# Linear attention and a SiLU feed-forward in one kernel: how the last 64 rows of each weight are loaded, and where four mask operations stand

## The chip, the cores and the metric

One core of a Trainium2 chip runs the whole program. The metric is the device time of one execution in microseconds. Engines are named as in the profile: PE (TensorE, matmuls and weight loads), DVE (VectorE), ACT (ScalarE), POOL (GpSimd), SP (SyncE, which here only issues transfers). Transfers are issued from two queues, SP's and ACT's, and run on 16 DMA engines.

## What is computed

```python
def _A_ref(x, wqkv, w_phi, wo):              # B=1, S=2048, D=448, H=16, Dh=28
    qkv = (x @ wqkv).reshape(B, S, 3, H, Dh).transpose(2, 0, 3, 1, 4)
    q, k, v = qkv[0], qkv[1], qkv[2]
    pq = einsum("bhsd,hdf->bhsf", q, w_phi)
    pk = einsum("bhsd,hdf->bhsf", k, w_phi)
    phi_q = concatenate([softmax(pq), softmax(-pq)], axis=-1)
    phi_k = concatenate([softmax(pk), softmax(-pk)], axis=-1)
    kv = einsum("bhsf,bhsd->bhfd", phi_k, v)
    z = einsum("bhsf->bhf", phi_k)
    num = einsum("bhqf,bhfd->bhqd", phi_q, kv)
    den = einsum("bhqf,bhf->bhq", phi_q, z)[..., None] + 1e-6
    o = num / den
    return o.transpose(0, 2, 1, 3).reshape(B, S, D) @ wo

def _B_ref(x, w1, w2):                       # w1 448 x 1792, w2 1792 x 448
    return silu(x @ w1) @ w2

xn = layernorm(x)
out = x + _A_ref(xn, wqkv, w_phi, wo) + _B_ref(xn, w1, w2)
```

All tensors are bfloat16.

## The kernel before

The 2048 tokens are worked on in eight pairs of 128-token tiles (`p` from 0 to 7). The depth of 448 is kept as seven blocks of 64 rows, and matmuls run as two half-array matmuls of 64 rows each, one on partitions 0 to 63 and one on 64 to 127 (`mm_448`, line 497). For that every weight stands in SBUF twice. The first 384 rows come in one load of 128 partitions times three blocks (`load_main`, line 566), and a copy of each half is written to the other half by DVE or ACT (`swap`, line 575; tile `w_sb` of the profile for w1). The last 64 rows, the tail, are loaded by `load_tail` (line 569) twice, once to partitions 0 to 63 and once to 64 to 127; no swap touches them.

The stages, in order: layer norm of a pair (`ln_pair`, line 672: statistics on DVE at line 621, the reciprocal root on POOL at 637, the normalised tile `xn_sb` at 650, a transpose on PE for pairs 0 to 3 at 508 and on the DMA for later ones); the first feed-forward product of pairs 0 to 3 (`ffn1_chunk`, 14 f-tiles of 128 columns, silu on ACT); the product of `w_phi` into wq and wk (`fold`); for each pair keys, values, their exponentials, sums and normalised features (`k_macro`, line 791), then one group of queries; every second pair the products of key features and values (`k_acc`, line 812); then the attention output, the second feed-forward product and wo. While PE has nothing to do at the start it multiplies zeros (`warm`, tile `zz`).

In `k_macro` the value copy out of PSUM is line 800 (DVE), the sums of the exponentials line 805 (DVE), their reciprocal 807 (DVE) and the product of features and reciprocal 808 (POOL). `k_acc` of pairs p-2 and p-1 stands behind the query group of pair p, for p of 2, 4 and 6, and reads the results of line 808.

The mask constants: POOL makes `maskh` (lines 524 and 527), DVE copies two columns of it to both halves of `mask2` (line 532, twice) and from there to the last column of `KVZ` (line 537, twice). They are read for the first time at line 862, when the key-value sums are done.

The order of work on each engine is not written out: each operation is recorded with its reads, writes, an assumed duration and a priority (`cur_prio`, 0 first), and `schedule` (line 218) plays the program through and picks operations by when they could start, by priority and by order of recording. For loads it reckons landing times ahead (`plan`, lines 247 to 272) from bytes and assumed rates, and adds 1700 ns to each. The order that comes out is fixed in the program; each engine then waits on semaphores. The loads of one queue are issued in the order of recording (lines 583 to 607): on SP x0, w1_0 (columns 0 to 255), x1, w1_0b (256 to 511), w1_1 (512 to 1023), the tail of columns 512 to 1791 as two loads, w1_2a (1024 to 1407), w1_2b (1408 to 1791), x2, x3, w_phi, then the transposed loads of wq and wk, x4 to x7, wv and its tail (`wvt`), wo's tail (`wot`); on ACT the two loads of the tail of columns 0 to 511. x0 is pair 0, x1 pair 1, and so on.

Of the kernel before, what the change touches and what calls it, by code (L numbers as in the profile page):

```python
# [144 lines left out]
class _Prog:  # L145
# [72 lines left out]
    def schedule(self):  # L218
        ops = self.ops
# [27 lines left out]
        plan = {}  # L247
# [5 lines left out]
        now, stalled = 0.0, False  # L253
        while loads["sp"] or loads["act"]:
            live = [e for e in ("sp", "act") if loads[e] and loads[e][0][2] <= now]
            nxt = [loads[e][0][2] for e in ("sp", "act") if loads[e] and loads[e][0][2] > now]
            if not live:
                now = min(nxt)
                continue
            cap = [190.0 if ops[loads[e][0][0]].half or ops[loads[e][0][0]].name == "wT_dt" else 310.0 for e in live]  # L260
            rates = [min(c, 310.0 * c / sum(cap)) for c in cap]
            step = min(min(loads[e][0][1] / r for e, r in zip(live, rates)), min(nxt) - now if nxt else 1e18)
            now += step
            if now > 2350.0 and not stalled:
                stalled = True
                now += 900.0
            for e, r in zip(live, rates):
                q = loads[e][0]
                q[1] -= step * r
                if q[1] <= 1.0:  # L270
                    plan[q[0]] = now + 1700.0
                    loads[e].pop(0)

        ndeps = [len(o.deps) + len(o.odeps) for o in ops]
# [25 lines left out]
        while done < n:  # L300
            cands = []
            tmin = None
            for e in ENGINES:
                for oid in ready[e]:
                    o = ops[oid]
# [11 lines left out]
            _, t, o = best  # L317
# [6 lines left out]
            if fill is not None:  # L324
                _, t, o = fill
# [39 lines left out]
def bass_parallel_sum__linear_kernel_hedgehog__dense_activation_silu__prompt_kernel(  # L365
# [10 lines left out]
    S, D, H, DH, FF = 2048, 448, 16, 28, 1792  # L376
# [9 lines left out]
    with es:  # L386
        def sb(name, shape, dt):
            return es.enter_context(nc.sbuf_tensor(name, shape, dt))
# [8 lines left out]
        w1_sb = sb("w1_sb", [128, KB, FF], BF16)  # L397
# [27 lines left out]
        KVZ = sb("KVZ", [128, 2, G, 2, DH + 2], BF16)  # L425
        kvs = sb("kvs", [128, 8 * 2 * (DH + 1)], F32)
        mask2 = sb("mask2", [128, 2], F32)
# [5 lines left out]
        maskh = sb("maskh", [KP, 4], F32)  # L433
# [30 lines left out]
        P = _Prog()  # L464
# [7 lines left out]
        def d_dve(n, mode=1):  # L472
            return n * 1.042 / mode + 150.0

        def d_rec(n):
            return n * 6.25 + 150.0

        def d_pool(n, per=1.0):
            return n * per + 120.0
# [34 lines left out]
        def act(dst, src, func, name, table=None, scale=1.0):  # L514
            return P.op("act", d_act(_cols(src)), lambda e: e.activation(dst, src, func, scale=scale),  # L515
                        reads=[src], writes=[dst], table=table, name=name)
# [4 lines left out]
             reads=[ones_bf[:]], writes=[ident[:]], name="ident")  # L521
# [4 lines left out]
             reads=[ones4[:]], writes=[mtmp[:]], name="mask1")  # L526
        P.op("pool", d_pool(4), lambda e: e.affine_select(maskh[:], mtmp[:], [[DH, 4]], ALU.is_ge, 0.0,
                                                           base=DH - 1, channel_multiplier=-1),
             reads=[mtmp[:]], writes=[maskh[:]], name="mask2")
        P.cur_prio = 2  # L530
        for r in range(2):
            P.op("dve", 150, lambda e, r=r: e.tensor_copy(mask2[64 * r:64 * r + 56, :], maskh[0:56, 0:2]),  # L532
                 reads=[maskh[0:56, 0:2]], writes=[mask2[64 * r:64 * r + 56, :]], name="mask3")
        for r in range(2):
            kvz_ones = KVZ[64 * r:64 * r + 56].rearrange("p s g h c -> p (s g) h c")[:, :, :, DH + 1]
            m2 = mask2[64 * r:64 * r + 56]
            P.op("dve", 150, lambda e, k=kvz_ones, m2=m2: e.tensor_copy(k, m2[:, None, :].broadcast_to([56, 8, 2])),  # L537
                 reads=[m2], writes=[kvz_ones], name="kvz1")
        wpad = W_sb[:, :, 0:QW].rearrange("p k (j f) -> p k j f", f=64)[:, :, :, 56:64]
        P.op("pool", d_pool(KB * 64), lambda e: e.memset(wpad, 0.0), writes=[wpad], name="wpad")  # L540

# [1 line left out]
        table_op = act(mtmp[:, 0:1], ones4[:, 0:1], ACTF.Silu, "table", table="silu")  # L543
# [10 lines left out]
        def load(dst, src, nbytes, name, eng="sp", keys_r=(), half=False):  # L554
            return P.dma(lambda e: e.dma_start(out=dst, in_=src), nbytes, writes=[dst], name=name, eng=eng, keys_r=keys_r, half=half, dur=580.0)
# [7 lines left out]
        def load_x(p0, p1, eng="sp"):  # L563
            load(x_sb[:, 2 * p0:2 * p1, :].rearrange("p (q t) d -> p q t d", t=2), xt[:, p0:p1], (p1 - p0) * 256 * D * 2, f"x{p0}", eng)

        def load_main(dst, src, c0, c1, d0, name):
            load(dst[:, 0:3, d0:d0 + c1 - c0], src[0:384, c0:c1].rearrange("(k p) f -> p k f", p=128), 384 * (c1 - c0) * 2, name)

        def load_tail(dst, src, c0, c1, d0, name, eng="sp"):
            for h in range(2):  # L570
                o = load(dst[64 * h:64 * h + 64, d0:d0 + c1 - c0], src[384:448, c0:c1], 64 * (c1 - c0) * 2, name, eng, half=True)
                if eng == "act":
                    o.odeps.add(table_op.id)

        def swap(dst, c0, c1, engs):
            for h in range(2):
# [6 lines left out]
        load_x(0, 1)  # L583
        load_main(w1_sb, B_w1, 0, 256, 0, "w1_0")
        load_tail(w1_sb[:, 6], B_w1, 0, 512, 0, "w1_0t", "act")
        load_x(1, 2)
        load_main(w1_sb, B_w1, 256, 512, 256, "w1_0b")
        load_main(w1_sb, B_w1, 512, 1024, 512, "w1_1")
        load_tail(w1_sb[:, 6], B_w1, 512, FF, 512, "w1_1t")
        load_main(w1_sb, B_w1, 1024, 1408, 1024, "w1_2a")  # L590
        load_main(w1_sb, B_w1, 1408, FF, 1408, "w1_2b")
        load_x(2, 3)
        load_x(3, 4)
# [126 lines left out]
        def exp_act(dst, src, scale, name):  # L720
            o = act(dst, src, ACTF.Exp, name, table="exp", scale=scale)
            for s in silus:
                if s.id not in o.deps:
                    o.odeps.add(s.id)
            exps.append(o)
# [61 lines left out]
        def k_unit(p, j, b0, name):  # L787
            mm_448([banks[b0 + t][:, 0:D] for t in range(2)], lambda h, k: xnT[:, k, p, :],
                   lambda h, k: W_sb[:, k, KO + (j - 1) * D:KO + j * D], True, True, name + "_mm", okeys_w=("late",) if p == NPAIR - 1 and j == 2 else ())

        def k_macro(p):
            sl = p % NEK
            k_unit(p, 1, 0, "pk")
            kb = psum[:, 0:1024].rearrange("p (t c) -> p t c", t=2)[:, :, 0:D]
            for s in range(2):
                exp_act(Ek[:, sl, :, s, :], kb, 1.0 if s == 0 else -1.0, "exp_k")
            k_unit(p, 2, 2, "v")
            vb = psum[:, 1024:2048].rearrange("p (t c) -> p t c", t=2)[:, :, 0:D].rearrange("p t (h d) -> p t h d", h=H)
            dstv = vaug[:, sl, :, :, 0:DH]
            P.op("dve", d_dve(896), lambda e: e.tensor_copy(dstv, vb), reads=[vb], writes=[dstv], name="v_ev")  # L800
            for ts in ((0, 2),) if p < NPAIR - 1 else ((0, 1), (1, 2)):
                n = ts[1] - ts[0]
                E3 = Ek[:, sl, ts[0]:ts[1], :, :].rearrange("p t s (h f) -> p (t s h) f", f=DH)
                S3, R3 = Sk[:, sl, 32 * ts[0]:32 * ts[1]], Rk[:, sl, 32 * ts[0]:32 * ts[1]]
                P.op("dve", d_dve(896 * n), lambda e, S3=S3, E3=E3: e.tensor_reduce(S3, E3, AXL.X, ALU.add),  # L805
                     reads=[E3], writes=[S3], name="Sk")
                P.op("dve", d_rec(32 * n), lambda e, S3=S3, R3=R3: e.reciprocal(R3, S3), reads=[S3], writes=[R3], name="Rk")  # L807
                P.op("pool", d_pool(896 * n, 1.77), lambda e, E3=E3, R3=R3, n=n: e.tensor_tensor(  # L808
                    E3, E3, R3[:, :, None].broadcast_to([128, 32 * n, DH]), ALU.mult),
                    reads=[E3, R3], writes=[E3], name="phik")  # L810
# [25 lines left out]
        for sl in range(NEK):  # L836
            P.op("pool", d_pool(32), lambda e, sl=sl: e.memset(vaug[:, sl, :, :, DH], 1.0),
                 writes=[vaug[:, sl, :, :, DH]], name="vaug1")
        for p in range(NPAIR):
            k_macro(p)  # L840
            if 1 <= p <= 5:
                P.keyw["early"] = exps[-1].id
                late_loads(p - 1)
            q_group(p // 4, p % 4)
            if p in (2, 4, 6):
                k_acc(p - 2, p)
# [3 lines left out]
        for r in range(2):  # L850
            lo, hi = 64 * r, 64 * r + 56
            src = [banks[4 + h][lo:hi, 0:464] for h in range(2)]
            dst = kvs[lo:hi, :]
            P.op("dve", d_dve(464), lambda e, src=src, dst=dst: e.tensor_copy(dst, src[0]), reads=[src[0]], writes=[dst], name="kvs")  # L854
            P.op("dve", d_dve(464), lambda e, src=src, dst=dst: e.tensor_tensor(dst, src[1], dst, ALU.add),  # L855
                 reads=[src[1], dst], writes=[dst], name="kvs2")
        for r in range(2):
            lo, hi = 64 * r, 64 * r + 56
            dst = KVZ[lo:hi, :, :, :, 0:DH + 1].rearrange("p s g h c -> p (s g) h c")
            src = kvs[lo:hi, :].rearrange("p (q h c) -> p q h c", q=8, h=2)  # L860
            m2 = mask2[lo:hi]
            P.op("dve", d_dve(464), lambda e, src=src, dst=dst, m2=m2: e.tensor_tensor(  # L862
                dst, src, m2[:, None, :, None].broadcast_to([56, 8, 2, DH + 1]), ALU.mult),
                reads=[src, m2], writes=[dst], name="kvz")
# [137 lines left out]
        p = NPAIR - 2  # L1002
# [7 lines left out]
        ops = P.ops  # L1010
# [12 lines left out]
        for e in ("pe", "act", "dve", "pool"):  # L1023
            cnt = 0
            for oid in order[e]:
                o = ops[oid]
# [4 lines left out]
        for e in ENGINES:  # L1031
            for oid in order[e]:
                o = ops[oid]
# [88 lines left out]
```

## Time and profile before

| | us |
|---|---|
| median of 3 runs | 158.16 |
| the runs | 158.72, 158.16, 157.37 |
| the profiled execution | 157.24 |
| its span in the profile | 155.5 |

| engine | busy us | share of the span |
|---|---|---|
| PE | 150.7 | 97% |
| PE weight loads | 98.3 | 63% |
| DVE | 102.6 | 66% |
| ACT | 74.2 | 48% |
| POOL | 63.7 | 41% |

The busy shares over 40 slices of 3.9 us each, with the DMA engines' (a digit is tenths, 9 is 90% or more):

```profile
PE   6889999999999999999999999999999999999994
DVE  5897977995978875889098769667985930022042
POOL 5320306379388775479601453366146060000000
PEclk9999999999999999999999999999999999999999
DMA  5999678303724223300000083300840143041011
```

Read these as averages over stages with different limits: PE is full from the third slice on, and the DMA engines are full in the first three slices. Two idle times are named in the view of waits: POOL waits 18.1 us in six pieces for DVE's line 635 in the first 30 us, and DVE waits 0.4 us for x to land.

### The profile page before, as it was taken

The page shows a single profiled execution, that of the slowest core. Times are in us where ns is not written, and L with a number is a line of the kernel's source. Part 1 is how long each engine was busy: PE and PEld are TensorE (multiplying, and loading weights), DVE is VectorE, ACT ScalarE, POOL GpSimd, SP SyncE. Part 2 cuts the span into 40 slices and gives each one's busy share as a digit, 9 for nine tenths or more (in the row PEclk, how much of TensorE's full clock was granted, in tenths as well). Part 3 has the DMA queues.
Part 4 walks back from the last instruction along what each step waited for, and adds up shares of the span by engine and source line. Part 5 has one row for each costly group of instructions (what it writes and reads, how often), then busy time and mean ns, then how long its engine had stood idle before and what let it go on. Part 6 is the DMA issues. An engine that isn't in the chain of part 4 may idle for free.

```text
span 155.5 us, 6049 instructions
## 1 busy us (share of the span) xinstructions
PE 150.7 (97%) x2751; PEld 98.3 (63%) x2751; DVE 102.6 (66%) x198; ACT 74.2 (48%) x82; POOL 63.7 (41%) x73
## 2 busy tenths in 40 slices
PE   6889999999999999999999999999999999999994
PEld 2378899795444546446878898655555555556553
DVE  5897977995978875889098769667985930022042
ACT  3778757878789688785955566800000000000000
POOL 5320306379388775479601453366146060000000
PEclk9999999999999999999999999999999999999999
DMA  5999678303724223300000083300840143041011
GB/s 152 268 277 115 110 180 249 62 17 69 99 53 139 49 93 95 93 0 6 4 4 4 0 63 63 59 4 0 124 118 4 28 115 98 0 118 63 0 59 59
DMA packets 23353, 12.11 MB, mean 78 GB/s; under 512 B 16160, under 2 KB 23200, under 8 KB 23328
## 3 DMA queue, kind: packets, MB, share of 16 engines
q1 hardware_dynamic: 23168, 11.60, 34.9%
q8 instruction: 21, 0.34, 0.9%
q10 hardware_dynamic: 160, 0.13, 0.3%
q14 instruction: 4, 0.03, 0.1%
HBM read 6.22 MB, written 1.84 MB: 52 GB/s over the span
## 4 chain that ended last, share of the span: by engine, by line
PE 89%; DVE 7%; POOL 2%; issue 1%; POOLq 0%
PE psum L490 84%; PE psum L483 4%; PE psum L508 1%; DVE st L621 1%; POOL rstd L637 1%; DVE KVZ L862 1%; DVE kvs L854 1%; DVE kvs L855 1%; DVE mask L532 1%; DVE xn_sb L650 1%; DVE mv L629 0%; DVE xnT L668 0%; DVE ve L635 0%; DVE KVZ L537 0%; POOL ident L519 0%
## 5 line engine op out<-in xcount | busy, mean ns | idle before, releaser
L490 PE MATMUL psum<-xnT,w_sb 64*128 64x256 bf16 (+1 forms) x1008 | 45.6, 246 | 0.5 <-DVE xn_sb L650 0.5
L490 PEld LDWEIGHTS psum<-xnT,w_sb 64*128 64x128 bf16 x1008 | 39.2, 94 | 5.0 <-ACT w_sb L515 0.6
L515 ACT ACTIVATE ar<-psum 128x896 bf16<-128x896 f32 (+2 forms) x38 | 32.0, 880 | 10.9 <-PE psum L490 10.8
L916 POOL TENSOR_TENSOR scr<-scr 128x384 bf16<-128x384 f32 (+3 forms) x32 | 20.1, 660 | 31.8 <-DVE scr L911 26.0
L808 POOL TENSOR_TENSOR ar<-ar,Rk 128x1792 bf16<-128x1792 bf16 (+1 forms) x9 | 25.8, 2877 | 10.1 <-DVE Rk L807 9.1
L960 DVE TENSOR_TENSOR out_sb<-psum,x_sb 128x448 bf16<-128x448 f32 (+2 forms) x17 | 9.5, 593 | 23.6 <-PE psum L490 20.5
L490 PE MATMUL psum<-ar,xnT 64*128 64x448 bf16 x224 | 22.7, 349 | 0.0
L490 PE MATMUL psum<-w_sb,hT_lo 64*128 64x448 bf16 x224 | 22.3, 349 | 0.0
L515 ACT ACTIVATE eq<-psum 128x1024 bf16<-128x1024 f32 x16 | 15.5, 1025 | 6.1 <-PE psum L490 6.0
L805 DVE TENSOR_REDUCE Sk<-ar 128x64 f32<-128x1792 bf16 (+1 forms) x9 | 16.2, 1804 | 2.5 <-ACT ar L515 2.5
L490 PEld LDWEIGHTS psum<-ar,xnT 64*128 64x128 bf16 x224 | 10.7, 94 | 10.4 <-DVE ar L800 0.4
L911 DVE TENSOR_TENSOR scr<-psum,Gq 128x896 f32<-128x896 f32 x16 | 16.9, 1087 | 0.4
L515 ACT ACTIVATE hT_lo<-psum 128x1024 bf16<-128x1024 f32 x14 | 14.3, 1022 | 5.9 <-PE psum L490 5.9
L490 PE MATMUL psum<-w_sb,ar 64*128 64x448 bf16 x168 | 16.6, 349 | 0.0
L490 PEld LDWEIGHTS psum<-w_sb,hT_lo 64*128 64x128 bf16 x224 | 10.5, 94 | 9.4
L637 POOL TENSOR_TENSOR rstd<-ve,neghalf 128x2 f32<-128x2 f32 (+1 forms) x9 | 6.2, 690 | 21.3 <-DVE ve L635 18.9
L490 PE MATMUL psum<-xnT,ar 64*128 64x512 bf16 x112 | 13.4, 376 | 0.0
L490 PEld LDWEIGHTS psum<-w_sb,ar 64*128 64x128 bf16 x168 | 8.4, 94 | 7.4
L490 PE MATMUL psum<-wo_sb,scr 64*128 64x448 bf16 (+2 forms) x119 | 11.9, 338 | 0.0
L800 DVE CAST ar<-psum 128x896 bf16<-128x896 f32 x8 | 8.6, 1069 | 4.0 <-PE psum L490 4.0
L621 DVE BATCH_NORM_STATS2 st<-x_sb 128x6 f32<-128x448 bf16 x16 | 9.7, 613 | 0.5 <-DMA x_sb<-in_A_x_dram 0.4
L650 POOL TENSOR_SCALAR xn_sb<-x_sb,mv,rstd 128x192 bf16<-128x192 bf16 (+1 forms) x8 | 9.5, 1190 | 0.4
(50 smaller groups left out, 119.4 us busy)
## 6 DMA issues: line engine op xcount, KB each, us to landing
out_dram<-out_sb SPq DMA_DIRECT2D x7, 224.0 KB, 2.2
x_sb<-in_A_x_dram SPq DMA_DIRECT2D x4, 224.0 KB, 5.4
x_sb<-in_A_x_dram SPq DMA_DIRECT2D x2, 448.0 KB, 4.8
w_sb<-in_B_w_dram SPq DMA_DIRECT2D x2, 448.0 KB, 3.6
w_sb<-in_B_w_dram SPq DMA_DIRECT2D x2, 336.0 KB, 3.4
w_sb<-in_B_w_dram SPq DMA_DIRECT2D x2, 288.0 KB, 6.6
w_sb<-in_B_w_dram SPq DMA_DIRECT2D x2, 192.0 KB, 3.4
w_sb<-in_B_w_dram SPq DMA_DIRECT2D x1, 384.0 KB, 6.5
```

Of the source, the lines that this page charges most:

```text
L483: lambda e: e.matmul(dst, lhsT, rhs, start=start, stop=stop, skip_group_check=True),
L490: r = e.matmul(dst, lhsT, rhs, start=start, stop=stop, skip_group_check=True)
L515: return P.op("act", d_act(_cols(src)), lambda e: e.activation(dst, src, func, scale=scale), reads=[src], writes=[dst], table=table, name= ...
L621: o = P.op("dve", 630, lambda e: e.bn_stats(st6[:, t, :], x_sb[:, t, :]), reads=[x_sb[:, t, :]], writes=[st6[:, t, :]], name="bnst")
L637: P.op("pool", 580, lambda e: e.tensor_tensor(r2, v2, nh, ALU.pow), reads=[v2, nh], writes=[r2], name="rstd")
L650: o = P.op("pool" if pool else "dve", 150 + _cols(xs) * 1.6 if pool else 120 + _cols(xs) * 0.6, lambda e, xn=xn, xs=xs: e.tensor_scalar(xn ...
L800: P.op("dve", d_dve(896), lambda e: e.tensor_copy(dstv, vb), reads=[vb], writes=[dstv], name="v_ev")
L805: P.op("dve", d_dve(896 * n), lambda e, S3=S3, E3=E3: e.tensor_reduce(S3, E3, AXL.X, ALU.add), reads=[E3], writes=[S3], name="Sk")
L808: P.op("pool", d_pool(896 * n, 1.77), lambda e, E3=E3, R3=R3, n=n: e.tensor_tensor(E3, E3, R3[:, :, None].broadcast_to([128, 32 * n, DH]), ...
L911: P.op("dve", d_dve(896), lambda e, dsto=dsto, Us=Us, Gs=Gs: e.tensor_tensor(dsto, Us, Gs[:, :, :, :, None].broadcast_to([128, 2, 2, 8, DH ...
L916: P.op("pool", d_pool(_cols(a0), 2.26), lambda e, dst=dst, a0=a0, a1=a1: e.tensor_tensor(dst, a0, a1, ALU.add), reads=[a0, a1], writes=[ds ...
L960: P.op("dve", d_dve(c1 - c0), lambda e: e.tensor_tensor(dst, ob, xs, ALU.add), reads=[ob, xs], writes=[dst], name="out_ev")
```

## The change

Three edits. `load_tail` issues one load in place of two: its destination is all 128 partitions, its source is the 64 rows under an outer dimension of 2 with step zero. Both queues use it, for w1, wv and wo. The tail of w1 that was loaded in two parts by columns (0 to 511 on ACT's queue, 512 to 1791 on SP's) is loaded in three (0 to 511 on ACT's; 512 to 1023 behind w1_1; 1024 to 1791 between w1_2a and w1_2b on SP's). The four DVE operations of the mask constants are recorded behind the third pair's `k_macro` and may not stand ahead of the first pair's value copy. The planner's constant for nine loads goes from 1700 to 2600 ns.

```diff
-                    plan[q[0]] = now + 1700.0
+                    plan[q[0]] = now + (2600.0 if ops[q[0]].name in ("w1_1", "w1_1t", "w1_2a", "w1_2b", "w1_2t", "x2", "x3") else 1700.0)
...
-        for r in range(2):
-            P.op("dve", 150, lambda e, r=r: e.tensor_copy(mask2[64 * r:64 * r + 56, :], maskh[0:56, 0:2]),
-                 reads=[maskh[0:56, 0:2]], writes=[mask2[64 * r:64 * r + 56, :]], name="mask3")
-        for r in range(2):
-            kvz_ones = KVZ[64 * r:64 * r + 56].rearrange("p s g h c -> p (s g) h c")[:, :, :, DH + 1]
-            m2 = mask2[64 * r:64 * r + 56]
-            P.op("dve", 150, lambda e, k=kvz_ones, m2=m2: e.tensor_copy(k, m2[:, None, :].broadcast_to([56, 8, 2])),
-                 reads=[m2], writes=[kvz_ones], name="kvz1")
...
         def load_tail(dst, src, c0, c1, d0, name, eng="sp"):
-            for h in range(2):
-                o = load(dst[64 * h:64 * h + 64, d0:d0 + c1 - c0], src[384:448, c0:c1], 64 * (c1 - c0) * 2, name, eng, half=True)
-                if eng == "act":
-                    o.odeps.add(table_op.id)
+            o = load(dst[:, d0:d0 + c1 - c0], src[384:448, c0:c1][None].broadcast_to([2, 64, c1 - c0]), 128 * (c1 - c0) * 2, name, eng)
+            if eng == "act":
+                o.odeps.add(table_op.id)
...
-        load_tail(w1_sb[:, 6], B_w1, 512, FF, 512, "w1_1t")
+        load_tail(w1_sb[:, 6], B_w1, 512, 1024, 512, "w1_1t")
         load_main(w1_sb, B_w1, 1024, 1408, 1024, "w1_2a")
+        load_tail(w1_sb[:, 6], B_w1, 1024, FF, 1024, "w1_2t")
         load_main(w1_sb, B_w1, 1408, FF, 1408, "w1_2b")
...
+        def late_masks():
+            for r in range(2):
+                P.op("dve", 150, lambda e, r=r: e.tensor_copy(mask2[64 * r:64 * r + 56, :], maskh[0:56, 0:2]),
+                     reads=[maskh[0:56, 0:2]], writes=[mask2[64 * r:64 * r + 56, :]], name="mask3").odeps.add(v_evs[0])
+            for r in range(2):
+                kvz_ones = KVZ[64 * r:64 * r + 56].rearrange("p s g h c -> p (s g) h c")[:, :, :, DH + 1]
+                m2 = mask2[64 * r:64 * r + 56]
+                P.op("dve", 150, lambda e, k=kvz_ones, m2=m2: e.tensor_copy(k, m2[:, None, :].broadcast_to([56, 8, 2])),
+                     reads=[m2], writes=[kvz_ones], name="kvz1")
+
+        v_evs = []
...
+            v_evs.append(P.ops[-1].id)
...
             k_macro(p)
+            if p == 2:
+                late_masks()
```

In the order that the planner makes of it, PE's instructions stand as before. On DVE the four mask operations stand between the first pair's value copy and its sums. On ACT the swap of columns 1408 to 1791 stands one place later, behind the silu of f-tiles 4 to 7. On DVE the statistics of pairs 4 to 7 change places among themselves.

## The prediction

> **What bounds the kernel now.** I read the page first (span 155.5 us, the run that was profiled took 157.24), then the chain of waits in order of time, then the DMA view and the table by windows for the first 14 us, and last the timeline around the place to which the mask constants go.
>
> ```profile
> PE 89%; DVE 7%; POOL 2%; issue 1%; POOLq 0%
> ```
> ```profile
> 2.01 0.93 DVE mask L532
> ...
> 3.40 0.20 DVE KVZ L537
> 3.60 0.03 issue
> 3.63 0.64 DVE st L621
> ...
> 10.23 0.39 DVE xn_sb L650
> 10.62 0.12 issue
> 10.74 1.35 PE psum L490 x42
> ...
> 18.43 0.50 PE psum L508 x7
> 18.93 3.23 PE psum L490 x112
> 22.16 0.50 PE psum L508 x7
> 22.66 51.56 PE psum L490 x1130
> ```
>
> TensorE carries 89% of the chain (first fence: the page's shares) and, in the chain itself (start, us, what), runs without a gap from 10.7 us on. Before that the chain goes through VectorE, and the loads stand behind it. So whatever makes TensorE stand still in the first 20 us is added to the end in full, and its order of instructions is the same in both kernels.
>
> The first 14 us belong to the loads (DMA view of 1.8 to 14 us; table by windows: span, busy time of five engines, clock, DMA share, GB/s):
>
> ```profile
> q10 hardware_dynamic: 160, 0.13, 3.9%
> ...
> x_sb<-in_A_x_dram SPq DMA_DIRECT2D x3, 224.0 KB, 6.9
> ...
> w_sb<-in_B_w_dram SPq DMA_DIRECT2D x2, 160.0 KB, 6.5
> ...
> w_sb<-in_B_w_dram ACTq DMA_DIRECT2D x2, 64.0 KB, 3.8
> ```
> ```profile
> 9.00:10.00 1.00, 1.00 (x43) 1.00 (x38) 0.93 (x4) 0.74 (x1) 0.60 (x1) 1.00 1.09 235
> 10.00:11.00 1.00, 0.55 (x22) 0.40 (x17) 0.86 (x5) 1.00 (x3) 0.19 (x1) 1.00 1.09 349
> ```
>
> All 16 DMA engines are full (share 1.09). Asked load by load, the trace gives issue plus time to landing: x0 0.8 + 2.4 = 3.2 us, the second half of w1's tail 4.1 + 6.5 = 10.6, x2 5.9 + 6.9 = 12.8, x3 6.4 + 7.0 = 13.4. The matmuls at 10.74 wait for that tail: TensorE was done with the four f-tiles before them at 10.3.
>
> **The change, part by part.**
>
> *The tail loads.* The old pair reads 64 rows and writes 64 partitions, twice. The new load reads the same rows under an outer loop of 2 with step zero and writes 128 partitions. Bytes are the same; what can differ is how the transfer is cut over the engines. No load of this trace has an outer loop below 64, so none shows it. The ends: cut in 16 as now, or cut in two, the only cut that the outer loops of both sides (2 and 128) share. I forecast two: one rule, "cut the outermost loop", describes every load of the trace (64, 112 and 128 are all multiples of 16) and leaves only two here.
>
> Then two engines carry all tails. Up to x3, an engine's sixteenth of the other loads is x0 14, w1_0 12, x1 14, w1_0b 12, w1_1 24, w1_2a 18, w1_2b 18, x2 14, x3 14 = 140 KB; the two also carry half of each tail, 64 + 64 + 96 = 224 KB. That is 364 KB against 168 now. Each queue's share on an engine goes in order, so x2 and x3 land behind it. Rate of one engine: this trace moved 168 - 14 KB (157.7 kB) per engine from x0's landing to x3's, 10.2 us: 15.5 B/ns. The ACT queue's tail rows took 3.9% of 16 x 12.2 us = 7.6 us for 0.131 MB: 17.2. The window 10 to 11 us gives 349/16/1.09 = 20.0, or 21.8 if the share is taken as 1. I take 20.0, as the other 14 engines fall silent early, and keep 15.5 and 21.8 as ends. After x0's landing 350 KB (358.4 kB) remain: 17.9 us, x3 at 21.1 us, x2 0.7 earlier at 20.4.
>
> What waits: VectorE's statistics of pair 2 (x2, then x3's first tile, in order). From the first of them (14.20) to the last xn (16.78 + 1.09 = 17.87) it is 3.67 us; begun at 20.4 it ends at 24.1, and the transposes that stood at 18.36 start then: **+5.7 us**. By the ends: x3 at 19.7, +4.3; x3 at 26.3, +10.8. The other path agrees: w1_2b, 28 KB before x3, lands at 19.7, its swap on ACT is 1.15, f-tiles 11 to 13 are half of the 4.69 us of matmuls: 23.2. Later loads (weights for the fold, x4, x6, wv) queue behind it on the two engines, but TensorE and VectorE are late by the same 5.7 us; I cost that at nothing, and if this cover is short, the high end has it.
>
> The Trainium skill ("DMA: Bandwidth & Descriptors", Rules for kernel authors) speaks against this change in these words: a leading zero-stride broadcast of c copies "confines the whole DMA to at most c engines". By that rule c is 2 and the sum is the one above; without it the sixteenths stay and the sum is that of the first rival.
>
> *One issue fewer.* ACT issues one load less (0.6 us), SP the same number up to w1_2b, and one less each at wvt and wot. The loads land 6.5 us after their issue, behind the data ahead of them, so an earlier issue gains nothing.
>
> *The masks leave the start.* x0 lands at 3.2 and its statistics start at 3.63, behind four mask operations; without them 0.4 us earlier. With the loads as forecast TensorE waits for w1 and x2 later on, so it is worth nothing; with 16 engines it is part of the rival's gain.
>
> *The masks leave for the stage of keys and values.* They are recorded behind the third pair, but in the built order they stand behind the first pair's value copy, ahead of the first sums; the planner fills an idle place with them. VectorE's and GpSimd's rows there:
>
> ```profile
> 38.01 2.31 POOL L650 TENSOR_SCALAR xn_sb<-x_sb,mv,rstd 128x192 bf16<-128x192 bf16 x2
> ...
> 38.55 1.08 DVE L800 CAST ar<-psum 128x896 bf16<-128x896 f32 x1
> ...
> 39.95 2.02 DVE L805 TENSOR_REDUCE Sk<-ar 128x64 f32<-128x1792 bf16 x1 [0.32 <-ACT ar L515]
> ```
>
> The four cost 0.16 + 0.16 + 0.20 + 0.20 and 0.1 between them, 0.8 us, into an idle 0.3: +0.5 for the sums. But the first mask copy took 0.93 us at the start where the second took 0.16: it ended at 2.94, with GpSimd's memsets. Here it starts at 39.63 while GpSimd normalises, until 40.32; held till then, the sums start at 41.1, +1.15. I take this end, since its row is that of the same instruction. Behind the waiting copy stand the sums and reciprocal of pair 0 (end 43.7), the value copy of pair 1 (44.8), its sums, which had an idle 0.9 ahead of them (46.8), and its reciprocal (47.4). GpSimd's product of pair 1 then runs 47.55 to 50.76 instead of 47.11 to 50.33. TensorE takes it up at 50.87: the cover is 0.5 us, and it holds, just. **Cost 0**; with the cover gone it would be the 1.15 at most. Pair 2's sums have 0.6 idle ahead of them, which takes the rest.
>
> The Trainium skill ("SBUF — State Buffer", Who interferes with whom) has it that VectorE in a two-port mode and GpSimd hold a shared port pair in turn, and the later one "fully blocks"; the row of 0.93 us agrees. The copies of weights at 26.50 (0.65 us beside GpSimd, 0.62 alone) do not; by either, the sum is the same.
>
> *The planner's constant* (2600 for 1700) moves orders alone: ACT's second 384-column swap behind the silu of f-tiles 4 to 7, statistics of pairs 4 to 7. f-tile 11 is 2.3 us behind f-tile 8, which covers a swap of 1.15 and a silu of 1.0: nothing.
>
> **Sum:** 157.24 + 5.7 + 0 = 162.9 for an execution like the profiled one; the median before, 158.16, is 0.9 above it. I predict 163.3, between the two. The forecast's own range goes from 157.2 + 4.3 = 161.5 to 157.2 + 10.8 = 168.0.
>
> **The rivals.**
>
> *Sixteen engines* (not slower). The tail of columns 512 to 1023 is 128 KB instead of 320, so it lands near 9.7 and f-tile 4 waits only for ACT's swap (10.1); TensorE resumes at 10.2 instead of 10.74, and statistics 0.4 us earlier carry it to the transposes of pair 2: -0.5 to -0.9, say -0.7: 156.5 (157.4 from the median). For it: today's 64-row loads land no later than the 128-row loads around them, and a cut at the second level would keep that. Against it: the outer loop is 2. It decides once the tail lands before 10.1.
>
> *Two engines, and the issuing queue stands behind them.* At 7.4 us, when the transposed loads begin to be issued, an engine of today has at most some 120 rows issued to it that it has not moved (w1_1 24, tails 8, w1_2a and w1_2b 24 each, x2 and x3 8 each, w_phi 28); the two would have over 240. If SP has to wait until they fall, near 18.8 when w1_2t lands, its six transposed loads (9.7 us of issuing, from 7.44 to 17.2 now) end at 28.5, x4 lands 4.4 later at 32.9, and its statistics, at 21.65 now, are late by 11.3: 168.5. For it: issues grew from 0.40 to 0.70 us at w1_1 and to 2.6 at the first transposed load. Against it: they fell back to 0.49 with more in the queue.
>
> *Not as described:* that the masks stand behind the first pair's values, not the third's, is in the sum; the tails are one load each in the built order. Nothing more is left of this than the cut.
>
> **How the numbers follow.** Two engines 0.65, two engines with a standing queue 0.15, sixteen 0.20. The range takes in most of the sixteen's (157) and goes up to 168.0, the forecast's end; outside lie the standing queue's half above it and the quick end of the first rival. About 1% (1.6 us) is what a measurement of this kernel can tell from no change: both two-engine cases lie above it, 0.80; the sixteen's -0.7 stays within it, 0.15, and a quarter of it goes past, 0.05.
>
> **What would show it.** Right: the tails' time to landing 10 us and more instead of 6.5, x3 near 21, a DMA share of about 0.13 (two of 16) in windows between some 10 and 20 us, gaps of TensorE before f-tiles 0, 4 and 8, transposes of pair 2 near 24; a first mask copy of 0.7 us or more and no gap ahead of the first key-value matmuls. Wrong: tails that land in 6.5 us or less, or a gap of TensorE with no load behind it, such as a lower granted clock after the waits, which no window of this trace shows.

## The result, and the profile after

| | before | after |
|---|---|---|
| median, us | 158.06 (6 runs, 157.12 to 158.72) | 163.93 (6 runs, 162.93 to 165.43) |
| the profiled execution, us | 157.24 | 162.93 |
| its span, us | 155.5 | 161.2 |
| mean granted clock in it | 1.0 | 0.989 |

The ratio, taken from the fast executions alone (that of 165.43 us is left out), is 1.0393, with a 95% interval of 1.0353 to 1.0434; the quotient of the medians is 1.037. The change costs about 6 us. The last matmul of the profiled execution stands 5.73 us later than before. The question is where these arise.

First the DMA view of 1.8 to 14 us (queue: packets, MB, share of 16 engines; then issues: count, KB each, median us from issue to landing), for the same window as in the prediction; the first line is of the kernel before, the others are of the changed kernel:

```profile
w_sb<-in_B_w_dram SPq DMA_DIRECT2D x2, 288.0 KB, 6.6
```
```profile
q10 hardware_dynamic: 130, 0.13, 3.5%
...
x_sb<-in_A_x_dram SPq DMA_DIRECT2D x3, 224.0 KB, 7.5
w_sb<-in_B_w_dram SPq DMA_DIRECT2D x2, 288.0 KB, 10.3
...
w_sb<-in_B_w_dram ACTq DMA_DIRECT2D x1, 128.0 KB
```

The first tail is one load of 128 KB now, and it shows no landing time, since the view looks for 16 completions. Asked load by load, the trace has three completion events for each tail load where it had 16 for each load before: one 1.1 to 1.4 us after the issue of w1's tails, then two. The last one counts: 9.12 us for the tail of columns 0 to 511 (w1_0t), 12.92 for 512 to 1023 (w1_1t), 17.82 for the rest (w1_2t). The two w1 loads of 288 KB, which are no tails, take 10.3 us to land, where they took 6.6. x2 lands at 19.18 and x3 at 19.84 (12.82 and 13.43 before).

The table by windows (span, busy time of five engines, clock, DMA share, GB/s; the share adds up the packets' times, so it can pass 1) shows the same from the engines' side; the two pairs of lines are from one-microsecond and two-microsecond windows:

```profile
9.00:10.00 1.00, 0.79 (x29) 0.82 (x31) 0.03 (x1) 0.44 (x2) 0.70 (x1) 1.00 0.14 47
10.00:11.00 1.00, 0.95 (x34) 0.77 (x28) 0.97 (x3) 1.00 (x2) 0.00 (x0) 1.00 0.14 47
```
```profile
14.00:16.00 2.00, 2.00 (x29) 1.51 (x25) 0.20 (x2) 0.76 (x1) 0.00 (x0) 0.57 0.81 220
16.00:18.00 2.00, 1.35 (x18) 0.70 (x16) 0.57 (x1) 1.02 (x1) 0.00 (x0) 0.58 1.29 61
```

From 9 to 11 us the share is 0.14, two of sixteen (2/16 is 0.125), at 47 GB/s where the same two windows of before had a share of 1.09 and 235 and 349 GB/s. The second pair shows the granted clock at 0.57 and 0.58, which no window of before shows.

What TensorE makes of it, in its timeline (start us, busy us, engine, line, operation, count, idle time before it and its releaser), before and after:

```profile
8.55 1.74 PE L490 MATMUL psum<-xnT,w_sb 64*128 64x128 bf16 x56
...
13.67 4.76 PE L490 MATMUL psum<-xnT,w_sb 64*128 64x256 bf16 x84
18.36 0.56 PE L508 MATMUL psum<-ident,xn_sb 128*128 128x128 bf16 x7
```
```profile
9.21 1.74 PE L490 MATMUL psum<-xnT,w_sb 64*128 64x128 bf16 x56 [0.97 <-DMA w_sb<-in_B_w_dram]
13.06 1.35 PE L490 MATMUL psum<-xnT,w_sb 64*128 64x128 bf16 x42 [2.11 <-DMA w_sb<-in_B_w_dram]
...
14.95 0.95 PE L508 MATMUL psum<-ident,xn_sb 128*128 128x128 bf16 x7
...
17.96 4.76 PE L490 MATMUL psum<-xnT,w_sb 64*128 64x256 bf16 x84 [0.65 <-ACT hT_lo L515]
22.95 0.56 PE L508 MATMUL psum<-ident,xn_sb 128*128 128x128 bf16 x7 [0.24 <-DVE xn_sb L642]
```

Matmul by matmul against before: f-tile 0 stands 0.65 us later (9.21), f-tile 4 2.31 (13.06), f-tile 8 4.28 (17.96), the transposes of pair 2 4.59 (22.95 for 18.36). Each f-tile starts just after a tail has landed. The line of f-tile 8 names ACT's `hT_lo`: that activation ended at 17.83 and w1_2t landed at 17.82, so the two waits end together. The tail alone would have held f-tile 8: in two other executions (e9 and e10 below) it starts 0.14 and 0.13 us behind the tail's landing, as it does here. The transposes of pair 1 at 14.95 took 0.95 us where they had taken 0.55: that is the low clock. It brings the lag to 3.35 us by 16.70, and costs nothing here, since f-tile 8 has to wait for its tail in any case.

After that the lag grows three times more: to 5.09 us at the value matmuls of 44.91 (39.81 before), to 5.49 at 49.46 (43.97 before), and to 5.73 at 80.02. The SyncE queue's timeline tells where the first of these comes from, before and after:

```profile
2.23 3.63 SPq L555 DMA_DIRECT2D w_sb<-in_B_w_dram  x6
5.91 1.01 SPq L555 DMA_DIRECT2D x_sb<-in_A_x_dram  x2
...
7.44 9.73 SPq L597 DMA_TRANSPOSE eq<-in_A_wqkv_dram  x6
...
17.21 0.58 SPq L555 DMA_DIRECT2D x_sb<-in_A_x_dram  x1
```
```profile
2.23 8.61 SPq L547 DMA_DIRECT2D w_sb<-in_B_w_dram  x6
10.88 1.91 SPq L547 DMA_DIRECT2D x_sb<-in_A_x_dram  x2
...
13.31 9.75 SPq L589 DMA_TRANSPOSE eq<-in_A_wqkv_dram  x6
23.10 1.15 SPq L547 DMA_DIRECT2D x_sb<-in_A_x_dram  x1
```

Six issues of w1 take 8.61 us in place of 3.63; single ones took 2.06 and 3.49 us, where none of w1's had taken over 0.70. So the first transposed load is issued at 13.31 for 7.44, and x4 at 23.10 for 17.21: it lands at 27.70, 6.07 us later than before, while TensorE is only 4.59 late. The last transposed load is issued behind it at 25.48 for 19.91 and lands at 30.00 for 25.08. VectorE waits for both, in its timeline before and after:

```profile
21.65 0.63 DVE L621 BATCH_NORM_STATS2 st<-x_sb 128x6 f32<-128x448 bf16 x1 [0.39 <-DMA x_sb<-in_A_x_dram]
...
25.20 0.23 DVE L736 COPY eq<-eq 112x256 bf16<-112x256 bf16 x1 [0.85 <-DMA eq<-in_A_wqkv_dram]
```
```profile
27.72 0.63 DVE L613 BATCH_NORM_STATS2 st<-x_sb 128x6 f32<-128x448 bf16 x1 [1.68 <-DMA x_sb<-in_A_x_dram]
...
30.08 0.23 DVE L728 COPY eq<-eq 112x256 bf16<-112x256 bf16 x1 [0.25 <-DMA eq<-in_A_wqkv_dram]
```

The second wait is the one that counts, at 30.08 for 25.20, 4.88 us late. From there the weight copies, statistics and normalised tiles of pairs 4 to 7 run on VectorE and GpSimd, and at their end stands pair 0's value copy, at 43.77 for 38.55, 5.22 us late. From the one copy to the other it is 13.70 us here, and 13.71 in the two experiments below that wait in the same way (e2 and e3), whenever x4 has landed; before it was 13.35, in the old order of VectorE's work. So about 0.35 of the 5.22 us belongs to the changed order, and 4.88 to the load. The chain of waits (start, us, what) has them, and the masks behind:

```profile
43.15 0.70 DVE xn_sb L642 x2
43.85 1.00 DVE ar L804
44.85 0.07 DVE mask L785
...
44.95 0.17 DVE mask L785
...
45.15 0.46 DVE KVZ L790
...
45.62 0.20 DVE KVZ L790
...
45.85 2.03 DVE Sk L810
...
49.46 30.26 PE psum L490 x705
```

The four mask operations take from 44.85 to 45.82, 1.0 us with their gaps, in front of the first sums. Of these 0.25 us is waiting: the first cast took 0.46 where the second took 0.20, and it ended 0.05 us behind this instruction of GpSimd, whose second half runs to 45.54:

```profile
43.22 2.31 POOL L642 TENSOR_SCALAR xn_sb<-x_sb,mv,rstd 128x192 bf16<-128x192 bf16 x2
```

TensorE's view of waits (in total, times, longest, us) has both in one line, 0.34 us at 44.91 and 0.22 at 49.46, beside the waits for the tails:

```profile
PE psum L490 <- DMA w_sb<-in_B_w_dram: 3.1, 2, 2.1
PE psum L508 <- DVE xn_sb L642: 1.6, 2, 1.3
...
PE psum L490 <- ACT hT_lo L515: 0.6, 1, 0.6
PE psum L490 <- DVE ar L804: 0.6, 2, 0.3
```

The last step, 0.24 us at 80.02, has the word "issue" in the chain; the same place moved by 0.25 us the other way in another kernel (the three parts alone), so it is taken for the spread of single executions.

### The profile page after: what moved, and what is told of

It is laid out like the page before. It is cut to its first block, busy times and chain, and to the rows that moved or that the text cites. A ratio compares the mean times of both kernels' runs of the same rounds, so it can differ in the third digit from the quotient of the medians.

```text
span 161.2 us, 6046 instructions
## 1 busy us (share of the span) xinstructions
PE 151.3 (94%) x2751; PEld 99.2 (62%) x2751; DVE 102.4 (63%) x198; ACT 74.4 (46%) x82; POOL 63.5 (39%) x73
## 4 chain that ended last, share of the span: by engine, by line
PE 65%; DVE 6%; POOL 2%; issue 1%
PE psum L490 62%; PE psum L483 3%; DVE Sk L810 1%; DVE ar L804 1%; POOL xn_sb L642 1%; DVE KVZ L869 1%; DVE kvs L861 1%; DVE kvs L862 1%; POOL rstd L629 0%; DVE xn_sb L642 0%; DVE KVZ L790 0%; DVE Rk L812 0%; DVE out_sb L967 0%; DVE mask L785 0%
## 5 line engine op out<-in xcount | busy, mean ns | idle before, releaser
L490 PEld LDWEIGHTS psum<-xnT,w_sb 64*128 64x128 bf16 x1008 | 40.0, 95 | 8.2 <-ACT hT_lo L515 3.4
L515 ACT ACTIVATE hT_lo<-psum 128x1024 bf16<-128x1024 f32 x14 | 14.3, 1021 | 7.6 <-PE psum L490 7.6
L490 PE MATMUL psum<-w_sb,ar 64*128 64x448 bf16 x168 | 16.6, 349 | 0.0
L515 ACT ACTIVATE w_sb<-w_sb 64x768 bf16<-64x768 bf16 (+1 forms) x8 | 7.3, 920 | 6.3 <-DMA w_sb<-in_B_w_dram 6.2
## 6 DMA issues: line engine op xcount, KB each, us to landing
w_sb<-in_B_w_dram SPq DMA_DIRECT2D x2, 288.0 KB, 10.3
```

The lines of the kernel that those rows point to most:

```text
L490: r = e.matmul(dst, lhsT, rhs, start=start, stop=stop, skip_group_check=True)
```

## The experiments

The theory: a tail load's outer dimension, now 2, decides on how many engines it runs, and the bytes on those two engines set when w1's tails and x3 arrive. The rivals: a source with step zero is slow by itself; the late masks cost; the three column parts or the issuing queue cost; only x2 and x3 being late matters.

**The tails as two loads of 64 rows again** (e1_pairs: the changed kernel with the old `load_tail`).

```diff
-            o = load(dst[:, d0:d0 + c1 - c0], src[384:448, c0:c1][None].broadcast_to([2, 64, c1 - c0]), ...)
+            for h in range(2):
+                o = load(dst[64 * h:64 * h + 64, d0:d0 + c1 - c0], src[384:448, c0:c1], ..., half=True)
```

> The changed kernel with each tail again as two loads of 64 rows, the three column parts, the late masks and the planner's constant kept. Theory (one load under an outer loop of 2 runs on two DMA engines): the whole loss goes; tails land some 6.5 us after issue, x3 near 13.4, transposes of pair 2 near 17.7, 157.0 to 157.6, at or a little below the kernel before. Rival (the three parts by columns, or the late masks, make most of the loss): 162 or more.

Measured 158.09 us, half a microsecond above what was expected, ratio 1.0015 (0.9974 to 1.0055): the loss is gone, with the masks, the three parts and the planner's constant still in. The DMA view of 1.8 to 14 us:

```profile
x_sb<-in_A_x_dram SPq DMA_DIRECT2D x3, 224.0 KB, 5.4
w_sb<-in_B_w_dram SPq DMA_DIRECT2D x2, 288.0 KB, 5.5
...
w_sb<-in_B_w_dram ACTq DMA_DIRECT2D x2, 64.0 KB, 3.7
w_sb<-in_B_w_dram SPq DMA_DIRECT2D x2, 64.0 KB, 5.3
```

The tails land in 3.7 to 5.3 us, the w1 loads behind them in 5.5 for 10.3, x3 at 13.19. So the form of the tail load carries the whole loss.

**The step of zero, with 16 and with 4 outer steps** (e2_outer16, e3_outer4: one load to 128 partitions as in the changed kernel, the same bytes moved; 56 and 32 of the tail's 64 rows are left out, so only the time is of use).

```diff
-            o = load(..., src[384:448, c0:c1][None].broadcast_to([2, 64, c1 - c0]), ...)
+            o = load(..., src[384:392, c0:c1][None].broadcast_to([16, 8, c1 - c0]), ...)
...
+            o = load(..., src[384:416, c0:c1][None].broadcast_to([4, 32, c1 - c0]), ...)
```

> The changed kernel, but each tail is one load of 8 of its 64 rows repeated 16 times, so the source has an outer loop of 16 with step zero; the other 56 rows are left out, the bytes moved and the instructions are the same. Theory (the outer count sets the engines): all 16 engines, tails land in 16 steps within 7 us of their issue, x3 near 13.2, 156.5 to 157.6. Rival (reading the same rows again under a step of zero is what is slow): tails land as late as in the changed kernel or later, 163 to 164.

> The same with 32 of the 64 rows repeated 4 times (outer loop of 4, the other 32 rows left out). Theory: four engines with 252 KB each up to x3 instead of 364 KB; at the 21.6 B/ns that the two engines of the changed kernel moved, x3 lands at 3.2 + 11.3 = 14.5 us, the last tail of w1 near 12.3; that is about what the statistics of pair 2 can bear, 157 to 159. Rival (step of zero is slow whatever the count): 163 to 164.

| engines a tail is on | kernel | completion events of a tail | x3 lands, us | KB per engine up to x3 | ratio to before |
|---|---|---|---|---|---|
| 16 | two 64-row loads | 16 | 13.19 | 168 | 1.0015 (0.9974 to 1.0055) |
| 16 | outer 16, step zero | 16 | 13.10 | 168 | 1.0001 (0.9966 to 1.0035) |
| 4 | outer 4, step zero | 5 | 16.36 | 252 | 1.020 (1.0138 to 1.0262) |
| 2 | the change | 3 | 19.84 | 364 | 1.0393 (1.0353 to 1.0434) |

The KB are those of the prediction's count: 140 for the other loads and 448 divided by the number of engines. Step zero alone costs nothing; the outer number decides. The Trainium skill ("DMA: Bandwidth & Descriptors", Why a DMA increments its semaphore by 16 and not by 1) says that a load on k engines has its semaphore raised by the remaining 16 - k at once and then by one for each engine. The events agree: one and two, one and four, sixteen.

The four engines were under-estimated: 160.7 us where 157 to 159 was expected. x3 lands 2.9 us late and pair 2's transposes stand only 1.6 late (19.96 for 18.36), but x4 is issued at 20.42 for 17.21, and the last transposed load lands at 27.53 for 25.08, 2.45 late. By pair 0's value copy (41.31 for 38.55) the lag is 2.6 to 2.8, and it ends at 3.64: 1.6 us from the tails, 1.0 at the value copy, 0.4 at the masks' place, and 0.6 in two steps further on that are not explained. What was expected had the first of these alone.

**The masks.** Once in the changed kernel put back at the start (e4_early_masks), once in the kernel before moved alone (e5_masks_only), and once more both kernels together on one chip (e9_after_again, e10_early_again).

```diff
         P.cur_prio = 2
+        for r in range(2):
+            P.op("dve", 150, lambda e, r=r: e.tensor_copy(mask2[64 * r:64 * r + 56, :], maskh[0:56, 0:2]),
...
             k_macro(p)
-            if p == 2:
-                late_masks()
```

That is the edit of the first and the fourth; the second makes the change's own edit of these lines in the kernel before, and the third is the changed kernel as it is.

> The changed kernel with the four mask operations back at the start. Theory (they cost 0.4 us at the value matmuls of pair 1, where TensorE's lag grew from 5.09 to 5.49, and gain nothing at the start because the loads are late): 163.5, TensorE's lag without that step. Rival (that step comes from the late loads alone): 163.9, the step stays. Second rival (the early start had gained its 0.4 us): 164.3.

> The kernel before with only the mask constants moved (four small VectorE copies and casts, now behind the first pair's value copy); loads as before. Theory (late masks put about 0.4 us in front of the first key-value sums and the earlier first statistics are mostly swallowed): 158.2 to 158.6 us where the kernel before reads 158.06, that is +0.1 to +0.5. Rival (the prediction's reading, covered and worth nothing): 157.9 to 158.2. Rival (the front gain of 0.4 us comes through): 157.5 to 157.8. In its trace the theory wants the four mask instructions between 39 and 41 us with the second one or a cast held for more than 0.4 us, and a TensorE wait for the key-value sums of 0.3 us or more that the trace of before does not have.

> The changed kernel as it is, on the same chip as the next run. Expected 163.2 to 164.6 us, ratio 1.036 to 1.043, with the third tail part landing at 17.5 to 19 us and x3 at 19.5 to 21.2.

> The changed kernel with the mask constants back at the start, beside the changed kernel on the same chip. If the late masks cost what they cost in the kernel before (0.6 us, interval 0.1 to 1.1), this is 0.3 to 0.9 us faster than the changed kernel. If the late loads swallow it (the key-value sums then wait for other things), both are within 0.3 us. If the masks at the start cost more, because they stand ahead of the first statistics while the loads arrive, it is 0.3 us or more slower, as one earlier look at it hinted (164.63 against 163.93 us, not on the same chip).

e4 read 164.63 us, ratio 1.0426 (1.0358 to 1.0494): not faster, but it was not run beside the changed kernel. e5 read 157.95 against 157.38, ratio 1.0038 (1.0009 to 1.0067): +0.6 us in the kernel before, somewhat more than any of the three expectations. The two kernels with sixteen engines that have the late masks too read 1.0015 (e1) and 1.0001 (e2), so +0.6 is at the upper end of what the times allow. The profiled execution of e5 was 1.3 us above its median, so its totals of waits are not read here; its mask operations took 0.34 and 0.62 us for the two copies and the two casts, as in the changed kernel (0.34 and 0.68). Side by side, the changed kernel read 163.99 us (1.0429, 1.0386 to 1.0471) and the one with early masks 163.74 (1.0424, 1.0383 to 1.0465). So the late masks cost at most about half a microsecond where the loads come in time, and nothing that can be measured on top of the late loads.

The traces show the cost at its place, the matmuls at 49.46 that wait for pair 1's value copy. There TensorE's lag grows by 0.2 to 0.4 us in all six executions with late masks in which the first cast was held (the change, e1, e2, e3, e5, e9). It grows by 0.02 in the seventh (e8), where GpSimd was done 0.24 us before the cast began and the cast took 0.19, and not at all in the four with early masks (e4, e6, e7, e10). In the six the cast ended 0.05 to 0.06 us behind GpSimd's instruction. That e10 is no faster for it has a reason in its trace: VectorE's copy behind the last transposed load stands at 31.16, 1.1 us later than in the change, and TensorE waits 0.88 us for pair 0's value copy, so the room that the masks leave is not used. That is one execution.

**The three column parts alone** (e6_parts_only: the kernel before with w1's tail in three parts, each two loads).

```diff
-        load_tail(w1_sb[:, 6], B_w1, 512, FF, 512, "w1_1t")
+        load_tail(w1_sb[:, 6], B_w1, 512, 1024, 512, "w1_1t")
         load_main(w1_sb, B_w1, 1024, 1408, 1024, "w1_2a")
+        load_tail(w1_sb[:, 6], B_w1, 1024, FF, 1024, "w1_2t")
```

> The kernel before with only the cut of w1's last 64 rows in three column parts, each still two 64-row loads, no masks moved, no planner constant. Theory (the parts cost two SyncE issues and bring f-tile 4's columns earlier, which the later wait for x3 swallows): 157.6 to 158.4 us, no change. Rival (the earlier f-tile 4 reaches the end, as its lag of -1.0 us in the pairs experiment hints): 157.0 to 157.6. Rival (two more issues push x2 and x3): 158.4 to 159.0 with x3 landing 0.3 us or more after 13.4.

157.32 us against 157.38 for the kernel before on the same chip, ratio 1.0009 (0.9984 to 1.0034). In its trace f-tile 4 stands 0.64 us earlier, and the last matmul 0.56. The medians hardly show it: the median span is 155.3 us for 155.6, but the time outside the span is 2.1 us for 1.8. It is 2.2 us in e1, the other kernel with two loads more, and 1.7 to 1.8 in all other runs; why is not shown.

**The tail form alone** (e7_tails_only: the kernel before with the new `load_tail`, and w1's columns 512 to 1791 still in one part).

> The kernel before with only the form of the load of the last 64 rows changed (one transfer to 128 partitions, source with a step of 0 outermost), w1's columns 512 to 1791 in one part, masks at the start, no planner constant. Theory (everything comes from two engines carrying each load): x3 lands between 19 and 21 us, three landing events per tail load, 163.0 to 165.0 us. Rival (part of the loss is the masks' or the three parts'): under 162.5 us. In its trace the theory wants the transposes of pair 2 between 22.5 and 24 us and the SyncE queue standing on its issues for 5 us or more before x2.

167.28 us, ratio 1.0612 (1.0573 to 1.065): worse than the whole change, and worse than expected. x3 lands at 20.56 as the theory wants (358.4 kB for each of the two engines in 17.2 us), but that is not what is waited for. TensorE's timeline:

```profile
9.83 1.74 PE L490 MATMUL psum<-xnT,w_sb 64*128 64x128 bf16 x56 [1.23 <-DMA w_sb<-in_B_w_dram]
17.87 2.42 PE L490 MATMUL psum<-xnT,w_sb 64*128 64x128 bf16 x42 [6.30 <-DMA w_sb<-in_B_w_dram]
```

f-tile 4 waits 6.30 us for a tail of 320 KB that lands at 17.73, because it needs the first columns of a load that counts only when all have come; and the clock is at half for some 6.8 us, from about 16.6 to 23.4 (f-tiles 4 to 6 take 2.42 us for 1.35). The lag is 7.12 us at f-tile 4 and 9.45 at f-tile 8. The cut in three parts, worth nothing with sixteen engines, saves about 3 us with two (ratio 1.0612 here and 1.0424 in e10, which has the three parts and early masks, and the planner's constant besides): TensorE works on f-tiles 4 to 7 while the third part still arrives. What was expected forgot this. The lower clock may be part of these 3 us: the mean granted clock is 0.979 in all six executions here and 1.0 in five of e10's six.

**x2 and x3 ahead of the second and third tail** (e8_x_first: the changed kernel with that order of issue, the third tail last of w1).

```diff
+        load_x(2, 3)
+        load_x(3, 4)
         load_tail(w1_sb[:, 6], B_w1, 512, 1024, 512, "w1_1t")
         load_main(w1_sb, B_w1, 1024, 1408, 1024, "w1_2a")
-        load_tail(w1_sb[:, 6], B_w1, 1024, FF, 1024, "w1_2t")
         load_main(w1_sb, B_w1, 1408, FF, 1408, "w1_2b")
-        load_x(2, 3)
-        load_x(3, 4)
+        load_tail(w1_sb[:, 6], B_w1, 1024, FF, 1024, "w1_2t")
```

> The changed kernel with x2 and x3 issued ahead of w1's second and third tail parts and the third tail last of w1; the same bytes on the same two engines. Theory (the bytes of the two engines set the end wherever they stand in the queue): x3 lands at 10.5 to 13 us, the third tail at 19 to 21 us, f-tile 8 waits for it instead of pair 2 waiting for x3, and the time stays at 163 to 165.5 us. Rival (only x2 and x3 being late hurts): x3 early brings 1.5 us or more back, 159 to 162.5 us.

165.26 us, ratio 1.0487 (1.0449 to 1.0524). x3 lands at 11.32 and pair 2 waits no longer, but the third tail lands at 19.79:

```profile
14.26 1.31 PE L490 MATMUL psum<-xnT,w_sb 64*128 64x128 bf16 x28 [1.92 <-DMA w_sb<-in_B_w_dram]
...
19.92 4.32 PE L490 MATMUL psum<-xnT,w_sb 64*128 64x256 bf16 x76 [1.90 <-DMA w_sb<-in_B_w_dram]
```

The two engines are done with the same bytes at 19.8 us in both orders. Only who waits last has changed, from pair 2's statistics to f-tile 8.

**What was not tried.** No kernel took the standing issues away and kept the two engines, so what is put down to them, and to the changed order, of the 0.5 us at the value copy rests on the traces. The planner's constant was not run alone; with it in, the kernel with two-load tails equals the kernel before. The lower clock was not switched off, but the record has executions without it. The four of e3 have a mean granted clock of 1.0 and are some 3 us slower than before, and the changed kernel's at 1.0 took 163.83 (above), 163.26 and 163.85 us (e9), no less than the 162.93 of the profiled one at 0.989. So the loss does not rest on it.

## Why the prediction was right, point by point

*What bounds the kernel.* Right: TensorE's gaps in the first 20 us came through to the end and none was recovered. (In the slices shown ahead of the prediction TensorE is full from the fourth on, not the third, and the DMA engines in the second to the fourth.)

*The tail loads in two engines.* Right in mechanism: three completion events, a DMA share of 0.14, and the loss gone with the pairs. The outer number alone decides (2, 4 and 16). The Trainium skill's rule ("DMA: Bandwidth & Descriptors", Rules for kernel authors, "at most c engines") agrees with all three. The same section advises against two transfers to partition halves, in favour of one 128-partition transfer; here two loads (1.0015) beat the change's one (1.0393), because that one has an outer number of 2; one load with an outer number of 16 (1.0001) is no worse than two.

*Its size* was off. The term took 20.0 B/ns for one engine and put x3 at 21.1 us and pair 2's transposes at +5.7. Measured: the 358.4 kB from x0's landing at 3.22 to x3's at 19.84 make 21.6 B/ns, close to the upper end of 21.8, and +4.59 us. From x2's landing to the transposes it took 3.77 us, for 3.67 taken. The other path, through w1_2b (18.61 for 19.7), was quicker too.

*Later loads, costed at nothing.* This step failed, by 0.50 us: TensorE was 4.59 us late, but the last transposed load held VectorE's copy 4.88 late, and with 0.35 from the changed order pair 0's value copy was 5.22 late and the value matmuls 5.09. The load was late for the reason of the third case, the standing issuing queue: it happened (8.61 us for six issues), earlier than was supposed, at w1's loads and x2, and then moved x4's issue by 5.9 us, not by 11.3. The case's price of 168.5 was wrong since the queue was free again at 13 us and not at 18.8.

*The masks, costed at nothing.* This step failed too, by 0.40 us in the trace. An operation was held until GpSimd's end as was said, but it was the first cast (0.46 us for 0.20) and not the first copy (0.15, beside GpSimd's running instruction), so the row of the same instruction at the start was no guide. Their place behind the first pair's value copy was right, and the sums were 1.0 us later for them, for 1.15 taken. What the working left out is a path: it followed pair 1 through its sums and GpSimd's product to TensorE at 50.87, with a cover of 0.5 us. But TensorE needs pair 1's value copy earlier, for the matmuls that stood at 43.97 before, and the working itself had moved the end of that copy from 43.5 to 44.8. In the changed kernel the matmuls at 49.46 wait for it, and TensorE's lag grew by 0.40. Alone the masks cost 0.6 us (0.1 to 1.1) by e5's ratio; in the changed kernel no difference was measured.

*One issue fewer, and the planner's constant, at nothing:* the first is borne out. The constant reaches seven loads of the changed kernel, not nine, and it may not be free: the changed order of VectorE's work takes 0.35 us more between the copy at 30.08 and the value copy, but it was not run alone. The gain of 0.4 us at the start was there (x0's statistics at 3.25 for 3.63) and was lost in the wait for w1_0t, as argued.

*The sum.* 5.7 + 0 was the measured 5.73, but by balance: the transfer term was 1.1 us too large, and the terms put at nothing came to 1.14 (0.50, 0.40 and 0.24, the last taken for spread). That 163.93 is so near to 163.3 rests on this balance; that it is 6 us and not zero or ten rests on the mechanism.

*The rivals.* Sixteen engines: its condition (the cut at the second level) is not met. Its price of -0.7 us was right as far as f-tile 4 (9.71 in e1 and 9.96 in e2, for 10.74), but the times don't have it: both intervals end above it (0.9974 and 0.9966 are -0.4 and -0.5 us). In e2's trace the lag of -0.78 us shrinks to -0.14 at the value matmuls, which wait for the same value copy (38.54 for 38.55). The lower clock, named as what would show the forecast wrong, came, and was hidden in the profiled execution. Of the signs named, a first mask copy of 0.7 us did not come.

## What to carry to other kernels

Before joining two loads into one, look at the outermost number of both sides: a source repeated c times in front runs on few engines when c is small, and every later load of the same queue waits behind its bytes on those engines. Keep many rows outermost, or leave two loads. When a load has become slow, cut it where its first reader needs it: the cut that was worth nothing at full width was worth about 3 us here. And when a load is late, look at the issuing queue too, since what stands behind it can be later still than the engine that seems to set the end.

## What was not expected of the hardware

Issues can stand with few engines in use: single issues of up to 3.49 us on SyncE in the change and of 1.06 to 1.68 us with four engines, where the kernel with two-load tails has none over 0.70 among the loads of w1, x2 and x3, and the one with a single load on sixteen engines none over 0.75. With fewer engines in use each was quicker: 15.8 to 16.3 B/ns for each of sixteen (157.7 kB from 3.45 or 3.20 us to 13.10 or 13.19), 19.0 for four (243.7 kB from 3.50 to 16.36), and 21.6 for two.

VectorE's first mask cast (56x16) met a running GpSimd instruction in six executions. Each time it took 0.39 to 0.45 us for 0.20 and ended 0.05 to 0.06 us behind that instruction. The copies of 56x2 just ahead of it, beside the same instruction, were not held (0.15 and 0.16 us). At the start, beside GpSimd's memsets, such a copy took 0.93.

After the waits the granted clock fell to one half though TensorE was working again. In another execution of the changed kernel it fell later, and cost time (table by windows: span, busy time of five engines, clock, DMA share, GB/s):

```profile
18.00:20.00 2.00, 1.32 (x24) 1.32 (x26) 0.59 (x2) 0.63 (x1) 0.00 (x0) 0.95 1.55 57
20.00:22.00 2.00, 2.00 (x22) 1.71 (x20) 1.90 (x6) 1.56 (x2) 0.18 (x1) 0.50 0.86 157
22.00:24.00 2.00, 2.00 (x30) 1.81 (x27) 1.90 (x7) 0.39 (x1) 0.51 (x1) 0.69 0.39 82
```

There it stretched f-tiles 8 and following by 1.6 us (lag 5.01 at 18.68, 6.60 at 23.13), and that execution took 164.39 us, for 162.93. Half-microsecond windows show the half clock from about 14.3 to 17.7 us in the first execution and from 19.7 to 23.2 in this one, some 3.4 us each. The Trainium skill ("TensorE: Matmul & The Clock Gate", What's actually happening) gives windows of about 3.4 us that run freely, after an idle one of which the clock is halved. The length agrees; the longest single idle time ahead of it was 2.11 us in the first execution and 2.6 in the other, with shorter ones around it, so that a whole idle window can't be read in these traces.
